# Omega on another issuing queue, the first loads in another order, and a planner that counts issue time: random-feature attention and two expert layers in fp32

## The chip, the cores and the metric

The kernel runs on one core of one Trainium2 chip. The metric is device time in microseconds of one execution. A core has TensorE (PE; matrix products and weight loads, PEld), VectorE (DVE), ScalarE (ACT), GpSimd (POOL) and SyncE (SP), and 16 DMA engines. Transfers are issued by an instruction on an engine's queue, here SyncE's and, for some, ScalarE's; in rows a queue is SPq or ACTq.

## The reference

```python
def _attn_ref(q, k, v, omega):            # q, k, v: (4, 8, 576, 64), omega: (128, 64)
    scale = 1.0 / np.sqrt(np.sqrt(D))
    def phi(x):                           # x = q * scale or k * scale
        proj = np.einsum('bhsd,md->bhsm', x, omega)
        h = proj - np.sum(x * x, axis=-1, keepdims=True) / 2.0
        return np.exp(h - np.max(h, axis=-1, keepdims=True)) / np.sqrt(m)
    kv = np.einsum('bhsm,bhsd->bhmd', phi(k * scale), v)
    z = np.sum(phi(k * scale), axis=2)
    num = np.einsum('bhsm,bhmd->bhsd', phi(q * scale), kv)
    den = np.einsum('bhsm,bhm->bhs', phi(q * scale), z)[..., None] + 1e-06
    return num / den
# x = attention output as (2304, 512)
gate = 1.0 / (1.0 + np.exp(-(x @ w_gate)))        # w_gate, w_val: (512, 1536)
x = (gate * (x @ w_val)) @ w_out                  # w_out: (1536, 512)
...
logits = x @ phi                                  # second layer: 8 experts of 4 slots
slot_input = softmax(logits, axis 0).T @ x
slot_out[e] = np.maximum(slot_input[e] @ w1[e], 0.0) @ w2[e]
return softmax(logits, axis 1) @ slot_out
```

## The kernel before, in words

Attention goes by 16 units of two heads. A unit has a transposed load of keys and queries (`QKTs`, two buffers; columns 0 to 511 keys, 512 to 639 the tails, the rest queries), a token-major load (`TOK`, one buffer, nine tiles: four of keys, one of tails, four of queries) and the values (`Vs`). `prep_first` and `prep_qk` square `TOK` and reduce the squares to one number for each row (`SQ`). `chunk_proj` multiplies 128 tokens at a time with Omega (`obf`, scaled once) into a PSUM bank, then VectorE subtracts the row's number and takes the minimum of the row (one instruction for a tile and head, which the rows of the trace call CUSTOM_DVE_ANT_0), and ScalarE takes the exponential. `chunk_kv`, `chunk_qT` and `chunk_num` make the attention output, which is stored in two float32r parts (`XT`).

The gated layer runs in 60 steps (`STEPS`: token block and 128 columns of the hidden layer), each three groups of twelve products: `ga`, `va` and the sum over the hidden layer in four banks `o0` to `o3`. Its weights come raw (`wall`, into four buffers `QS`), are converted by ScalarE, VectorE and GpSimd (`convert`), spilled to DRAM (`wscr`) and read again in later blocks (`load_w`, into `ws`); each is split into two float32r parts just before use (`split_w`). The second layer follows in chunks between the steps and at the end.

Nothing is issued in the order in which it is written. `Plan` records every instruction with its dependencies and a due time; `schedule` runs a list schedule over five engines, with the prices of `cost`, and this gives the order of each engine's queue. A recorded instruction may name two engines; the schedule picks one. SyncE's and ScalarE's queues run in order, so a transfer that waits for a buffer holds what stands behind it. All instructions are issued by one helper, so that all rows show its line, L403.

The lines that the change touches are the end of `cost` (before: an issue on SyncE costs 0.06, one on ScalarE what an elementwise instruction of that size costs), the table `PARTS` of `chunk_proj`, and the first lines that are recorded, L1109 to L1139. A call of `chunk_proj` takes one bank for a part of fewer than four tiles.

Of the kernel before, what the change touches and what calls it, by code (L numbers as in the profile page):

```python
# [101 lines left out]
class Plan:  # L102
# [95 lines left out]
    def cost(self, eng, method, kw, outs, ins):  # L198


        if method == "together":
            return TURN * (kw["parts"][0][2][0].ap[0][1] == 64) + sum(self.cost(eng, a[1], a[3], o, i)[0] for a, o, i in kw["parts"]), False
        o = outs[0] if outs else None
        n = self.free(o) if o is not None else 0
        if eng == "PE":
            if method == "transpose":
                return 0.109 * max(0.5, o.ap[0][1] / 128), False
            if ins[0].dtype == F32R:
                return (n + 32) / 2400.0, False
            if o.ap[0][1] == 32:  # L210
                return max(0.43 * n / 256, 0.055) / 4, False
            if o.ap[0][1] == 64:
                return max(n / 600.0, 0.21) / 2 + 0.12, False
            return (max(0.222, n / 600.0) / 2 if ins[0].ap[0][1] == 64 else max(0.222, n / 600.0)), False
        ni = max([n] + [self.free(a) for a in ins])
        psum = any(a.space == bass.MemoryType.PSUM for a in ins + outs)
        if eng == "ACT":
            return (0.07 if psum else 0.11) + 0.00083 * ni + 0.09 * sum(self.free(a) == 1 for a in ins), False
        if eng == "DVE":
            if method == "reciprocal":  # L220
                return 0.06 + 0.0054 * n, False
            if method == "tensor_tensor_reduce":
                return 0.075 + ni / 960.0, False
            if method == "tensor_reduce" or psum:
                return 0.067 + ni / 960.0, False
            if method in ("tensor_tensor", "scalar_tensor_tensor"):
                return 0.067 + ni / 960.0, True
            return 0.067 + ni / 1920.0, method != "memset"
        if eng == "POOL":
            return 0.1 + 0.00225 * ni, True  # L230
        return 0.06, False
# [174 lines left out]
def body(ctx, tc, nc, qkT, tok, von, omT, wall, phi, w1, w2, ident_d, srep_d, rrep_d, mask_d, out):  # L406
    plan = Plan(nc)
    PE, ACT, DVE, POOL, SP = (Eng(plan, e) for e in ("PE", "ACT", "DVE", "POOL", "SP"))
# [23 lines left out]
    def warm(x, n, tag):  # L432

        ps = bank(tag)[:, 0:x.shape[-1]]
        for _ in range(n):
            PE.matmul(ps, x[:, 0:128], x, start=True, stop=True)
# [7 lines left out]
    def stream(name, t):  # L444
        plan.t = t
        plan.lead = LEAD[name]
# [22 lines left out]
    def carve(reg, at, shape):  # L469
        n = int(np.prod(shape))  # L470
        names = "abcde"[:len(shape)]
        v = reg[:, at:at + n]
        if len(shape) == 1:
            return v
        return v.rearrange(f"p ({' '.join(names)}) -> p {' '.join(names)}",
                           **{c: d for c, d in zip(names, shape)})
# [14 lines left out]
    QKTs = [carve(g2, 1152 * k, [1152]) for k in range(2)]  # L491
    TOK = carve(g2, 2304, [9, 2, D])
    Vs = [carve(g3, 1280 * k, [NT, 2, 128]) for k in range(2)]
    QTF = carve(g3, 2560, [2, S])
    obf = carve(g3, 3712, [256])
    HKs = [carve(r, 0, [4, 2, M]) for r in (g4, q2)]
# [10 lines left out]
    def turn(lst, name):  # L507
        ring[name] = ring.get(name, -1) + 1
        return lst[ring[name] % len(lst)]
# [4 lines left out]
    def bank(tag=None):  # L514
        if tag is None:
            tag = turn(FLW, "fl") if wide[0] else "fl"
        tag = "fl" if tag in POOLED else tag
        return plan.tile(psp, [128, 512], F32, tag, NFL if tag == "fl" else 1, dyn=tag == "fl")
# [22 lines left out]
    def prep_first(a, e):  # L541

        w = SQW[:, 2 * a:2 * e, :]
        y = TOK[:, a:e].rearrange("p t h d -> p (t h) d")
        ACT.activation(out=w, in_=y, func=AF.Square)
        DVE.tensor_reduce(out=SQ[:, 2 * a:2 * e], in_=w, axis=AX.X, op=ALU.add)

    PARTS = {"K": (0, 4, HKs, 0, 0), "K0": (0, 2, HKs, 0, 0), "K1": (256, 2, HKs, 2, 4),
             "T": (512, 1, HTs, 0, 8), "Q": (640, 4, HQs, 0, 10), "Q0": (640, 2, HQs, 0, 10), "Q1": (896, 2, HQs, 2, 14)}

    def chunk_proj(u, i):

        if u >= NU:
            return
        c0, nt, hb, t0, g0 = PARTS[i]
        hb = hb[u % 2][:, t0:t0 + nt]
        x = QKTs[u % 2][:, c0:c0 + 128 * nt]
        if nt < 4:
            both = bank()[:, 0:256 * nt].rearrange("p (t h m) -> p t h m", h=2, m=M)
            ps = [both[:, :, h] for h in range(2)]  # L560
        else:
            ps = [bank()[:, 0:128 * nt].rearrange("p (t m) -> p t m", m=M) for _ in range(2)]

        def products():
            for t in range(nt):
                if nt < 4:
                    PE.matmul(both[:, t].rearrange("p h m -> p (h m)"), x[:, 128 * t:128 * t + 128], obf,
                              start=True, stop=True)
                    continue
                for h in range(2):  # L570
                    r = slice(64 * h, 64 * h + 64)
                    PE.matmul(ps[h][:, t], x[r, 128 * t:128 * t + 128], obf[r, 128 * h:128 * h + 128],
                              start=True, stop=True)

        plan.together(products, [SQ[:, g0:g0 + 2 * nt]], [hb])
        low = turn(MX, "mx")
        for h in range(2):
            for t in range(nt):
                g = 2 * t + h
                DVE.tensor_tensor_reduce(out=hb[:, t, h], in0=ps[h][:, t],  # L580
                                         in1=SQ[:, g0 + g:g0 + g + 1].to_broadcast([128, M]),
                                         scale=1.0 / 16.0, scalar=BIG, op0=ALU.add, op1=ALU.min,
                                         accum_out=low[:, g:g + 1])
        for h in range(2):
            for t in range(nt):
                g = 2 * t + h
                ACT.activation(out=hb[:, t, h], in_=hb[:, t, h], func=AF.Exp, scale=-1.0, bias=low[:, g:g + 1])
# [519 lines left out]


    stream("att", T0)  # L1109
    ACT.preload_act_table_set("natural_log_exp_and_others")  # L1110
    DVE.memset(g4[:, 0:256], 0.0)
    warm(g4[:, 0:256], W0N, "va")
    for h in range(2):
        r = slice(64 * h, 64 * h + 64)
        DVE.memset(obf[r, 128 * (1 - h):128 * (2 - h)], 0.0)
        SP.dma_start(out=obf[r, 128 * h:128 * h + 128], in_=omT[r])
    SP.dma_start(out=TOK[:, 0:2], in_=tok[0][:, 0:2])
    SP.dma_start(out=QKTs[0][:, 0:256], in_=qkT[0][:, 0:256])
    SP.dma_start(out=TOK[:, 2:5], in_=tok[0][:, 2:5])
    SP.dma_start(out=QKTs[0][:, 256:640], in_=qkT[0][:, 256:640])  # L1120
    SP.dma_start(out=QKTs[0][:, 640:1152], in_=qkT[0][:, 640:1152])
    SP.dma_start(out=TOK[:, 5:9], in_=tok[0][:, 5:9])
    SP.dma_start(out=QKTs[1], in_=qkT[1])
    SP.dma_start(out=Vs[0], in_=von[0])
    SP.dma_start(out=ident, in_=ident_d)
    DVE.memset(one_b, 1.0)
    DVE.memset(den_b, 1e-6)
    DVE.tensor_scalar(out=obf, in0=obf, scalar1=-16.0 * float(D ** -0.25), scalar2=None, op0=ALU.mult)
    prep_first(0, 2)
    chunk_proj(0, "K0")  # L1130
    prep_first(2, 5)
    prep_qk(0, 1)
    chunk_proj(0, "K1")
# [176 lines left out]
def build(nc, arrays):  # L1310
    args = [nc.dram_tensor(n, a.shape, mybir.dt.from_np(a.dtype), kind="ExternalInput").ap()
            for n, a in arrays.items()]
    args.append(nc.dram_tensor("out_0", (NTOK, DM), F32, kind="ExternalOutput").ap())
    with tile.TileContext(nc, schedule_with_timeline_sim=True) as tc:
        with ExitStack() as ctx:
            body(ctx, tc, nc, *args)
# [8 lines left out]
```

## Time and profile before

| | |
|---|---|
| median of 3 runs | 694.21 us (693.05 to 696.72) |
| the profiled execution, its own time | 696.61 us |
| its span, first to last instruction | 694.8 us |
| PE busy | 668.5 us, 96% of the span |
| DVE busy | 459.4 us, 66% |
| ACT busy | 433.1 us, 62% |
| POOL busy | 288.4 us, 42% |
| transfers | 139.49 MB, mean 201 GB/s |

The shares are means over the whole span. Stages differ: attention alone at first, then attention beside the first steps of the gated layer, then the gated layer alone with chunks of the second one, then the end of the second layer. A matmul counts as busy while it waits in the array's pipeline, so a busy PE is not PE at its peak.

### The profile page before, as it was taken

To read this page: it belongs to the slowest core of one execution; us is meant where nothing else is said; L and a number is where in the kernel's file an instruction comes from. 1 tells how busy PE (TensorE), PEld (TensorE's weight loads), DVE (VectorE), ACT (ScalarE), POOL (GpSimd) and SP (SyncE) were. 2 spreads that over 40 slices of the span, in tenths; PEclk is the share of its full clock that TensorE was granted. 3 is DMA by queue.
4 is the path that set the end of the run, shared out by engine and by line. 5 is a ranking of instruction groups with operands and counts; after the bars stand their busy time and mean duration, and the time that the engine had idled before them with its cause. 6 is when DMAs were issued, how large, how long until landed. Compare 5 with 4: busy or idle time off the path is not lost.

```text
span 694.8 us, 12218 instructions
## 1 busy us (share of the span) xinstructions
PE 668.5 (96%) x4217; PEld 535.4 (77%) x4217; DVE 459.4 (66%) x1304; ACT 433.1 (62%) x968; POOL 288.4 (42%) x244
## 2 busy tenths in 40 slices
PE   7899899999999999999999999999999999999993
PEld 5676577778787888888788888788888789998562
DVE  3899999899997476766566664566454335765221
ACT  5899788888787665765667675454444446764021
POOL 0565445575344334344444543444444444642000
PEclk9999999999999999999999999999999999999898
DMA  7989766777965345424353312689432338658996
GB/s 253 327 273 334 258 213 226 266 249 249 320 221 178 125 136 195 152 90 125 119 186 118 92 46 92 205 291 342 147 92 92 107 86 290 175 163 265 329 389 215
DMA packets 50125, 139.49 MB, mean 201 GB/s; under 512 B 5520, under 2 KB 11152, under 8 KB 50064
## 3 DMA queue, kind: packets, MB, share of 16 engines
q1 hardware_dynamic: 45456, 121.94, 52.9%
q10 hardware_dynamic: 4608, 16.78, 7.1%
q8 instruction: 33, 0.54, 0.3%
q14 instruction: 28, 0.23, 0.1%
HBM read 124.54 MB, written 14.16 MB: 200 GB/s over the span
## 4 chain that ended last, share of the span: by engine, by line
PE 79%; DVE 8%; DMA 5%; ACT 3%; issue 3%; SPq 1%; POOL 0%; POOLq 0%; ACTq 0%; DVEq 0%
PE o L403 25%; PE ga L403 20%; PE va L403 19%; PE fl L403 15%; DVE x2T L403 3%; DVE g L403 2%; DMA ws<-wscr 2%; DMA g<-in_wall 2%; DVE x L403 1%; ACT g L403 1%; DMA wscr<-x 1%; DMA g<-in_tok 1%; ACT ga_a L403 1%; SPq L403 1%; DVE gt L403 1%
## 5 line engine op out<-in xcount | busy, mean ns | idle before, releaser
L403 POOL TENSOR_TENSOR w<-ws,w 128x512 fp32r<-128x512 f32 x138 | 181.6, 1317 | 254.1 <-ACT w L403 156.4
L403 PE MATMUL ga<-XT,w 128*128 128x512 f32 (+1 forms) x720 | 168.5, 376 | 0.7 <-DVE ga_a L403 0.7
L403 PE MATMUL o<-gt,w 128*128 128x512 f32 (+1 forms) x720 | 167.8, 377 | 0.9 <-ACT w L403 0.8
L403 PE MATMUL va<-XT,w 128*128 128x512 f32 (+1 forms) x720 | 166.9, 375 | 0.0
L403 PEld LDWEIGHTS o<-gt,w 128*128 128x128 f32 x720 | 123.6, 189 | 26.5 <-issue 3.9
L403 PEld LDWEIGHTS va<-XT,w 128*128 128x128 f32 x720 | 123.8, 189 | 25.4 <-issue 4.1
L403 PEld LDWEIGHTS ga<-XT,w 128*128 128x128 f32 x720 | 123.6, 189 | 25.5 <-DVE ga_a L403 1.3
L403 ACT ACTIVATE w<-ws 128x512 fp32r<-128x512 f32 x108 | 67.8, 627 | 58.4 <-PE o L403 19.5
L403 PE MATMUL fl<-g,g 64*128 64x128 f32 (+4 forms) x686 | 84.1, 313 | 4.8 <-DVE g L403 4.2
L403 ACT ACTIVATE g<-g 128x128 f32<-128x128 f32 (+3 forms) x204 | 73.4, 410 | 15.3 <-DVE g L403 9.7
L403 ACT ACTIVATE ga_a<-ga_a 128x512 f32<-128x512 f32 (+1 forms) x120 | 69.9, 583 | 20.4 <-DVE ga_a L403 19.5
L403 PEld LDWEIGHTS fl<-g,g 64*128 64x128 f32 (+2 forms) x686 | 61.0, 183 | 26.7 <-DVE g L403 9.4
L403 ACT ACTIVATE ga_a<-ga 128x512 f32<-128x512 f32 (+1 forms) x60 | 33.2, 553 | 67.0 <-PE ga L403 66.8
L403 DVE SCALAR_TENSOR_TENSOR ga_a<-ga,ga_a 128x512 f32<-128x512 f32 (+1 forms) x60 | 38.1, 634 | 41.0 <-ACT ga_a L403 40.9
L403 DVE CAST w<-ws 128x512 fp32r<-128x512 f32 x54 | 23.1, 428 | 57.5 <-PE ga L403 37.5
L403 ACT ACTIVATE x2T<-g 128x512 f32<-128x512 f32 x72 | 45.5, 665 | 8.2 <-DVE x L403 7.8
L403 DVE TENSOR_TENSOR ga_a<-va,ga_a 128x512 f32<-128x512 f32 (+1 forms) x60 | 38.0, 634 | 15.5 <-ACT ga_a L403 9.9
L403 ACT ACTIVATE g1b<-g1b,g 128x128 f32<-128x128 f32 x128 | 40.5, 390 | 8.6 <-DVE g L403 8.6
L403 DVE TENSOR_SCALAR x2T<-x2T 128x512 f32<-128x512 f32 (+1 forms) x72 | 44.0, 627 | 1.0 <-ACT x2T L403 1.0
L403 DVE TENSOR_TENSOR gt<-ga_a,gt 128x512 fp32r<-128x512 f32 (+1 forms) x53 | 40.3, 760 | 2.3 <-ACT gt L403 1.3
L403 ACT ACTIVATE ga_a<-ga_a,one_b 128x512 f32<-128x512 f32 (+1 forms) x60 | 40.7, 678 | 1.4
L403 DVE TENSOR_TENSOR g<-fl,g 64x288 f32<-64x288 f32 (+3 forms) x61 | 29.3, 482 | 17.4 <-ACT g L403 16.5
(201 smaller groups left out, 787.7 us busy)
## 6 DMA issues: line engine op xcount, KB each, us to landing
ws<-wscr SPq DMA_DIRECT2D x42, 512.0 KB, 3.6
ws<-wscr SPq DMA_DIRECT2D x78, 256.0 KB, 2.8
g<-in_wall SPq DMA_DIRECT2D x36, 512.0 KB, 4.5
g<-in_von SPq DMA_DIRECT2D x16, 640.0 KB, 5.2
wscr<-x SPq DMA_DIRECT2D x36, 256.0 KB, 4.1
g<-in_qkT SPq DMA_DIRECT2D x15, 576.0 KB, 4.9
g<-in_tok SPq DMA_DIRECT2D x15, 576.0 KB, 5.0
g<-in_w ACTq DMA_DIRECT2D x16, 512.0 KB, 6.1
```

The costliest lines, as they stand in the source:

```text
L403: getattr(self.eng[e], method)(*a, **k)
```

## The change

Omega's two loads are issued on ScalarE's queue instead of SyncE's, ahead of the activation table load, which was ScalarE's first instruction. SyncE starts with the token-major load; the last four token tiles come one place earlier, before the last part of keys and queries; the second unit's key and query load comes after the values and the identity. The first part of the projection, two key tiles in one bank (`K0`), becomes two parts of one tile, with a bank each (`Ka`, `Kb`). In the planner a transfer's issue costs 0.5 on SyncE and 0.06 on any other engine.

```diff
@@ cost
+        if method == "dma_start":
+            return 0.5 if eng == "SP" else 0.06, False
         o = outs[0] if outs else None
@@ PARTS
+             "Ka": (0, 1, HKs, 0, 0), "Kb": (128, 1, HKs, 1, 2),
@@ body
     stream("att", T0)
-    ACT.preload_act_table_set("natural_log_exp_and_others")
     DVE.memset(g4[:, 0:256], 0.0)
     warm(g4[:, 0:256], W0N, "va")
+    SP.dma_start(out=TOK[:, 0:2], in_=tok[0][:, 0:2])
     for h in range(2):
         r = slice(64 * h, 64 * h + 64)
         DVE.memset(obf[r, 128 * (1 - h):128 * (2 - h)], 0.0)
-        SP.dma_start(out=obf[r, 128 * h:128 * h + 128], in_=omT[r])
-    SP.dma_start(out=TOK[:, 0:2], in_=tok[0][:, 0:2])
+        ACT.dma_start(out=obf[r, 128 * h:128 * h + 128], in_=omT[r])
     SP.dma_start(out=QKTs[0][:, 0:256], in_=qkT[0][:, 0:256])
     SP.dma_start(out=TOK[:, 2:5], in_=tok[0][:, 2:5])
     SP.dma_start(out=QKTs[0][:, 256:640], in_=qkT[0][:, 256:640])
+    SP.dma_start(out=TOK[:, 5:9], in_=tok[0][:, 5:9])
     SP.dma_start(out=QKTs[0][:, 640:1152], in_=qkT[0][:, 640:1152])
-    SP.dma_start(out=TOK[:, 5:9], in_=tok[0][:, 5:9])
-    SP.dma_start(out=QKTs[1], in_=qkT[1])
     SP.dma_start(out=Vs[0], in_=von[0])
     SP.dma_start(out=ident, in_=ident_d)
+    SP.dma_start(out=QKTs[1], in_=qkT[1])
+    ACT.preload_act_table_set("natural_log_exp_and_others")
...
-    chunk_proj(0, "K0")
+    chunk_proj(0, "Ka")
+    chunk_proj(0, "Kb")
```

The planner's new prices reach every queue. Three places follow. The first is the start of SyncE's queue. In these rows `g_78` holds `TOK` and `QKTs` (128x256, 128x384 and 128x512 are the parts of the first unit, 128x1152 a whole unit), `g_79` holds Omega and the values, `in_wall` are raw weights. Before:

```order
L403 DMA g_79<-in_omT 64x128 x2
L403 DMA g_78<-in_tok 128x256
L403 DMA g_78<-in_qkT 128x256
L403 DMA g_78<-in_tok 128x384
L403 DMA g_78<-in_qkT 128x384
L403 DMA g_78<-in_qkT 128x512
L403 DMA g_78<-in_tok 128x512
L403 DMA g_78<-in_qkT 128x1152
L403 DMA g_79<-in_von 128x1280
L403 DMA ident<-in_ident 128x128
L403 DMA g_79<-in_von 128x1280
L403 DMA g_78<-in_tok 128x1152
```

The same queue after the change:

```order
L405 DMA g_78<-in_tok 128x256
L405 DMA g_78<-in_qkT 128x256
L405 DMA g_78<-in_tok 128x384
L405 DMA g_78<-in_qkT 128x384
L405 DMA g_78<-in_tok 128x512
L405 DMA g_78<-in_qkT 128x512
L405 DMA g_79<-in_von 128x1280
L405 DMA ident<-in_ident 128x128
L405 DMA g_78<-in_qkT 128x1152
L405 DMA g_79<-in_von 128x1280
L405 DMA g_78<-in_tok 128x1152
L405 DMA g_75<-in_wall 128x1024 x2
```

Omega's two issues are gone, the 128x512 part of the tokens has moved from eighth to fifth, and the second unit's token load (128x1152) is now followed by two weight loads where four stood.

The second place is the start of ScalarE's queue. `g_78` 128x256, 128x384, 128x512 and 128x640 are squares of token tiles, `g_80` 128x128 exponentials of a tile and head, `fl` and `o` PSUM banks. Before:

```order
L403 ACT_TABLE_LOAD
L403 ACTIVATE g_78<-g_78 128x256
L403 ACTIVATE g_78<-g_78 128x384
L403 ACTIVATE g_80<-g_80 128x128 x18
L403 ACTIVATE g_80<-o_88 128x256
L403 ACTIVATE g_79<-o_90 128x2x256
L403 ACTIVATE g_79<-fl 128x2x256
L403 ACTIVATE g_79<-o_93 128x2x64
L403 ACTIVATE g_80<-fl,den_b 128x288
```

The same queue after the change:

```order
L405 DMA g_79<-in_omT 64x128 x2
L405 ACT_TABLE_LOAD
L405 ACTIVATE g_78<-g_78 128x256
L405 ACTIVATE g_78<-g_78 128x384
L405 ACTIVATE g_80<-g_80 128x128 x2
L405 ACTIVATE g_78<-g_78 128x512
L405 ACTIVATE g_80<-g_80 128x128 x16
L405 ACTIVATE g_80<-fl 128x256
L405 ACTIVATE g_79<-o_93 128x2x256
L405 ACTIVATE g_79<-o_94 128x2x64
L405 ACTIVATE g_78<-g_78 128x640
L405 ACTIVATE g_80<-o_100,den_b 128x288
```

The square of the last four token tiles (128x512) and that of the second unit's first five (128x640) have come from GpSimd to ScalarE, and one PSUM copy has gone to VectorE.

The third place is SyncE's queue late in the first blocks of the gated layer, where raw weights, spills (`wscr`) and reloads (`ws`, 128x1024 for the two input weights, 128x512 for the output weight) alternate. Before:

```order
L403 DMA wscr<-x_138 128x512
L403 DMA ws<-wscr 128x1024
L403 DMA g_75<-in_wall 128x1024
L403 DMA wscr<-x_138 128x512
L403 DMA ws<-wscr 128x512
L403 DMA g_75<-in_wall 128x1024
```

The same place after the change:

```order
L405 DMA ws<-wscr 128x1024
L405 DMA wscr<-x_139 128x512
L405 DMA g_75<-in_wall 128x1024 x2
L405 DMA wscr<-x_139 128x512
L405 DMA ws<-wscr 128x512
L405 DMA ws<-wscr 128x1024
```

Between the two reloads of one step stand two raw weight loads and two spills now, where one of each stood.

## Rows read from the trace of the kernel before

**Rows 1.** Busy time by stage: stretch, its length, then each engine's busy time.
```profile
0.00:20.00 20.00, 15.29 (x69) 11.62 (x70) 6.98 (x46) 10.46 (x27) 2.50 (x6) 1.00 0.79 269
20.00:150.00 130.00, 124.71 (x770) 90.28 (x769) 122.71 (x440) 114.44 (x297) 72.52 (x65) 1.00 0.77 265
150.00:210.00 60.00, 57.43 (x276) 46.71 (x274) 59.25 (x106) 49.05 (x98) 27.57 (x20) 1.00 0.77 258
210.00:625.00 415.00, 414.14 (x2415) 346.67 (x2416) 248.49 (x655) 244.07 (x514) 181.94 (x150) 1.00 0.48 152
```

**Rows 2.** The chain of waits at the start: start, duration, what.
```profile
4.54 6.02 DMA g<-in_tok
10.70 1.05 POOL g L403
...
13.09 7.00 DMA g<-in_wall
```

**Rows 3.** Timeline of SyncE's queue, first 12 us: start, duration, issue.
```profile
0.73 1.24 SPq L403 DMA_DIRECT2D g<-in_omT  x2
2.01 0.59 SPq L403 DMA_DIRECT2D g<-in_tok  x1
...
3.12 0.43 SPq L403 DMA_DIRECT2D g<-in_tok  x1
...
4.54 0.43 SPq L403 DMA_DIRECT2D g<-in_tok  x1
...
6.44 0.88 SPq L403 DMA_DIRECT2D g<-in_von  x1
11.76 0.33 SPq L403 DMA_DIRECT2D g<-in_tok  x1
```

**Rows 4.** Transfers of the first 40 us: GB/s by us; issue to landing in us.
```profile
GB/s 0 0 57 181 227 291 237 262 319 324 284 404 381 386 328 311 295 281 397 422 420 415 441 402 386 215 243 333 128 188 378 361 398 164 319 316 316 278 108 161
...
g<-in_qkT SPq DMA_DIRECT2D x1, 256.0 KB, 4.6
g<-in_tok SPq DMA_DIRECT2D x1, 256.0 KB, 6.0
...
g<-in_tok SPq DMA_DIRECT2D x1, 128.0 KB, 2.4
```

**Rows 5.** Timeline of the first 20 us, all engines; in brackets idle time and releaser.
```profile
0.73 1.28 ACT L403 ACT_TABLE_LOAD   x1 [0.73 <-PEq L1320]
...
5.38 2.05 PE L403 MATMUL fl<-g,g 128*128 128x256 f32 x4 [1.27 <-DVE g L403]
...
7.47 0.29 DVE L403 CUSTOM_DVE_ANT_0 g<-fl,g 128x128 f32<-128x128 f32 x1
...
18.39 1.25 POOL L403 TENSOR_TENSOR g<-g 128x640 f32<-128x640 f32 x1 [6.65 <-DMA g<-in_tok]
...
19.68 0.82 DVE L403 TENSOR_REDUCE g<-g 128x10 f32<-128x640 f32 x1 [5.31 <-POOL g L403]
```

**Rows 6.** Groups of instructions by shape, whole span: count, busy us, mean ns.
```profile
L403 DVE CUSTOM_DVE_ANT_0 x<-x2T 128x1024 uint16<-128x1024 uint16 x25 | 24.3, 971 | 0.1
L403 DVE CAST gt<-ga_a 128x512 fp32r<-128x512 f32 x37 | 23.9, 647 | 0.8
L403 DVE TENSOR_TENSOR w<-ws,w 128x512 fp32r<-128x512 f32 x24 | 18.0, 750 | 5.4 <-ACT w L403 4.5 <-issue 0.5
L403 DVE COPY g<-fl 128x512 f32<-128x512 f32 x13 | 8.9, 686 | 2.3 <-PE fl L403 2.2
L403 ACT ACTIVATE g<-g 128x512 f32<-128x512 f32 x8 | 5.0, 626 | 2.2 <-DVE g L403 1.3 <-issue 0.9
L403 ACT ACTIVATE g<-g 128x640 f32<-128x640 f32 x2 | 1.5, 732 | 0.7 <-DVE g L403 0.7
```

**Rows 7.** Waits of SyncE's queue: what it waited for: us, times, longest.
```profile
SPq L403 <- DVE x2T L403: 87.4, 39, 7.9
```

**Rows 8.** SyncE's loads of the tile ws: who waited for them (us, times).
```profile
  POOL w L403: 2.2, 1
  DVE w L403: 0.2, 1
```

## The prediction

> **What bounds the kernel now.** I read first the busy time by stage [rows 1]. From 210 to 625 us TensorE is busy 414.14 of 415 us: there the time is its own work, and nothing that arrives earlier shortens it; it can only start earlier. From 20 to 210 us VectorE is the fullest engine, 122.71 of 130 and 59.25 of 60 us, with TensorE at 124.71 and 57.43; both carry a backlog. In the first 20 us nobody is full: VectorE 6.98, ScalarE 10.46, TensorE 15.29 us. So idle time in the first 20 us is paid in full at the end, unless a later stage has a bound of its own.
>
> Then the chain of waits [rows 2]. It starts on SyncE's queue, runs through one transfer of 6.02 us (the last four tiles of the token-major load, `TOK[:, 5:9]`), GpSimd's square of it, and from there into a 7.00 us weight load. The queue itself [rows 3] shows why: SyncE issues its first load at 0.73 us, needs about 0.6 us for each of the first and 0.43 to 0.47 us from start to start later, and issues nothing between 7.3 and 11.76 us, because the next unit's token load overwrites `TOK` and waits for that square. The timeline [rows 5] shows what it costs: the square ends at 11.75 us and VectorE reduces it next; the next unit's square starts at 18.39 us, when its load has landed, 6.63 us after its issue, and VectorE, idle 5.31 us, gets its reduction at 19.68 us. The first product waits until 5.38 us.
>
> **The change, part by part.**
> Omega to ScalarE's queue. Two issues leave SyncE: its first token load moves from 2.01 to 0.73 us, 1.28 us [rows 3]. Omega keeps its issue times, now on an idle engine. The activation table load goes behind it, so by the same issue times it begins at about 2.0 instead of 0.73 us and, at its 1.28 us [rows 5], ends at 3.3; the first square needs a token load issued at 0.73 us, and that load lands 2.4 us after issue [rows 4], at 3.1 us, where it lands at 4.4 now. Cost 0.2 us on a square that still starts 1.1 us sooner: nothing on the path. Without that cover it would be 1.3 us.
>
> Order of the first loads. `TOK[:, 5:9]` was the eighth issue of the queue (4.54 us) and is now the fifth, which is issued at 3.12 us today [rows 3]. The 256 KB load that stands where it will stand among the large loads (the last part of the key and query load) landed 4.6 us after issue, `TOK[:, 5:9]` itself 6.0 us [rows 4]. So it lands at 3.1 + 4.6 = 7.7 us, at worst 9.1, instead of 10.56. Its square is on ScalarE in the new order: 0.63 us [rows 6] in place of 1.05 [rows 2]. ScalarE's two exponentials ahead of it are of tile 0, long done. The square ends at 8.4 us (worst 9.8) instead of 11.75, and the next token load is issued then: 3.4 us sooner (worst 1.9).
>
> That gain doesn't arrive whole, because the transfers are then bound by traffic. All that is issued up to and with that load is, by the shapes in the code, 3712 KB or 3.8 MB. The figures of [rows 4], one per us, add to 4.7 MB when it lands today at about 18.3 us: 0.9 MB of the four weight loads issued behind it went first. In the new order two weight loads stand behind it, then a load that waits for TensorE, so I take between 0.45 and 0.9 MB. The same sums, 4.25 to 4.7 MB, are reached at 16.9 to 18.3 us today and 1.28 us sooner after the change: 15.6 to 17.0, a gain of 1.3 to 2.7. I take 2.0. The square behind it moves from GpSimd (1.25 us [rows 5]) to ScalarE (0.73 us [rows 6]): 0.5 more. So the second unit's reduction comes at about 17.2 us instead of 19.68: 2.5 us, bounds 1.8 and 3.2. What lies ahead has room: the first unit's last reduction on VectorE moves from 11.8 to about 8.5 us, and what queues behind it moves too.
>
> The Trainium skill, DMA: Bandwidth & Descriptors, section "Issuing engines are not separate DMA queues", says that transfers issued from different engines run on the same 16 DMA engines and interleave, so that several issuers save only issue time. It speaks against the move of Omega as a gain in bandwidth. The trace agrees as far as it goes: from 11 us on the figures of [rows 4] stay between 281 and 422 GB/s with one queue issuing. By that rule alone the change would give its 1.28 us of issue time and no more.
>
> The last part of the key and query load stands one place later now; it may land at 3.6 + 6.0 = 9.6 us instead of 8.6. VectorE then still has the reductions of earlier tiles queued ahead of its own, at 0.29 us for one half tile [rows 5]: 0, at most the 1 us if that queue were empty.
>
> A bank for each of the first two key tiles. VectorE's first row reduction at 7.47 us waits for both tiles of one bank, 2.05 us of product [rows 5]; with a bank each it needs one tile, half of that. Its key load, the fourth issue today, is the second now, so the first product can start about 1.3 us sooner, near 4.1 us, and VectorE near 5.2. That work sits in front of the wait for the second unit's load, so it is hidden by it: 0. If that load came at once, it would be worth up to 2 us.
>
> The counted issue. SyncE's issue costs 0.5 us in the plan instead of 0.06, ScalarE's 0.06 instead of the price of an elementwise operation. This reorders every engine. TensorE's matmuls are the same 3376. Counted in the orders up to the nineteenth gate step, about where VectorE stops being the bound, VectorE loses five PSUM copies (0.69 us each) and three conversion adds (0.97), 6.3 us, and gains four subtractions (0.75), two casts of the gated value and two of weights (0.65 at most each), 5.6 us [rows 6]. Net 0.7 us less; 0 if what waits there is TensorE, up to 2 with the small copies, which I leave out. I take 0.7 us. ScalarE gains four squares of 128x640 (0.73 each) and some of the copies.
>
> Sum: 2.5 + 0.7 = 3.2 us. Span 694.8 - 3.2 = 691.6 us; the profiled execution's own time 696.61 becomes 693.4. It lies 2.4 us above the median of the runs, 694.21, which becomes 691.0 us. About 0.5% (3.5 us) is what a measurement of this kernel tells from no change, so this lies just inside it.
>
> **Rivals.**
> *Carried, and the new order closes more.* VectorE idles 7.3 us and TensorE 5.3 us between 20 and 150 us [rows 1]. An order planned with true issue times may place loads sooner and close half of VectorE's part, 3.6 us: 687.4. For it: the chain is made of loads that come late. Against: after 20 us SyncE mostly waits for buffers, not for its issue.
>
> *Not carried.* The start gains only the issue time, 1.28 us, or the stage up to 150 us hides the rest, since ScalarE is busy 114.44 of its 130 us and now gets more: 692.9 to 694.2. The first of these is also what the Trainium skill's rule on issuing engines, above, gives.
>
> *Slower: a reload queued behind weight loads.* SyncE's queue is in order. In the new one, a reload of the output weights (`ws`, 128x512) stands behind two raw weight loads, where one stood before. Each of these waits for a buffer that VectorE's conversion must free; such waits reached 7.9 us [rows 7]. If the reload comes that late and the step waits, the time is 691.0 + 7.9 = 698.9. It decides once the reload is later than its slack. Against it: of 120 reloads two were waited for, 2.4 us in all [rows 8].
>
> **How the numbers follow.** Forecast case 0.50, with its own range 689.0 to 692.9 (3.2 + 2.0, and 1.3 with nothing from the order); a little over half of it lies past the 0.5% bound at 690.7. Closing more 0.18, not carried 0.15, slower 0.17. Faster by over 0.5%: 0.26 + 0.18 = 0.44. Within: 0.24 + 0.15 = 0.39. Slower: 0.17. The range 686.5 to 696.5 leaves out the dear half of the slower case and the tail of the gain.
>
> **What would show it.** The first token load issued near 0.7 us and the first product near 4.1; `TOK[:, 5:9]` landed by 7.7 to 9.1; the next token load issued near 8.4; the second unit's reduction on VectorE near 17.2; TensorE's full stretch beginning about 3 us sooner, with the same length of 415 us. I am wrong if the start is 2.5 us ahead and TensorE's idle time between 20 and 250 us has grown by as much, if ScalarE is what VectorE waits for between 20 and 100 us, or if waits for `ws` appear before the weight splits.

## The result, and the profile after

The change made the kernel slower. The median is 703.02 us (698.60 to 705.04, 9 runs) against 694.35 us (693.05 to 697.96, 9 runs); the ratio, taken over all runs and not of the two medians (which lie 8.7 us apart), is 1.0095, with a 95% interval of 1.0071 to 1.0118: 6.6 us slower, at least 4.9, where 3.2 us faster was forecast, and outside the forecast's range.

The profiled execution of the changed kernel is its fastest (698.60 us, span 696.7), so its span lies only 1.9 us above before's 694.8. Part of the rest is the clock at the end: between 640 and 661 us the granted clock was 0.84 before and 1.00 after. The steps in the middle compare better. TensorE's seventeenth gate step begins at 247.70 us before and at 252.83 after.

First the start. SyncE's queue after (start, duration, issue), which answers to [rows 3]:

```profile
0.74 0.41 SPq L405 DMA_DIRECT2D g<-in_tok  x1
...
2.71 0.43 SPq L405 DMA_DIRECT2D g<-in_tok  x1
...
5.10 0.56 SPq L405 DMA_DIRECT2D g<-in_von  x1
7.93 0.33 SPq L405 DMA_DIRECT2D g<-in_tok  x1
```

The timeline of the other engines, for [rows 5]:

```profile
1.96 1.28 ACT L405 ACT_TABLE_LOAD   x1 [1.96 <-issue]
...
5.00 1.22 PE L405 MATMUL fl<-g,g 128*128 128x256 f32 x2 [0.89 <-DVE g L405]
...
14.85 0.74 ACT L405 ACTIVATE g<-g 128x640 f32<-128x640 f32 x1
...
15.62 0.82 DVE L405 TENSOR_REDUCE g<-g 128x10 f32<-128x640 f32 x1 [1.43 <-ACT g L405]
```

The first token load goes out at 0.74 us, `TOK[:, 5:9]` at 2.71, the next unit's token load at 7.93 instead of 11.76, and the second unit's reduction comes at 15.62 instead of 19.68 us. All of this is as soon as forecast or sooner, except the first product: 5.00, not 4.1. The chain of waits says why (start, duration, what):

```profile
0.74 0.55 ACTq L405
...
1.32 3.20 DMA g<-in_omT
```

Omega's second half landed 3.20 us after its issue at 1.32, and the scaling on VectorE had to wait for it.

So the start is 4 us ahead. Now the busy time by stage, for [rows 1] (stretch, length, then PE, PEld, DVE, ACT, POOL, granted clock, DMA share, GB/s):

```profile
0.00:20.00 20.00, 16.90 (x81) 12.79 (x82) 11.04 (x68) 14.23 (x37) 2.23 (x7) 1.00 0.87 323
20.00:150.00 130.00, 123.30 (x753) 88.69 (x754) 114.43 (x409) 114.94 (x296) 66.81 (x60) 1.00 0.75 256
150.00:210.00 60.00, 57.16 (x272) 45.78 (x271) 57.37 (x112) 47.13 (x94) 26.36 (x20) 1.00 0.79 262
210.00:625.00 415.00, 412.87 (x2383) 344.46 (x2382) 239.49 (x637) 246.02 (x519) 182.85 (x152) 1.00 0.46 150
```

VectorE, nearly full before, is now idle 15.57 of 130 us between 20 and 150, where it was idle 7.29. It has less to do, and TensorE still does 1.41 us less than before in that stretch, 0.27 less in the next and 1.27 less in the last. TensorE's timeline after shows some of the places; in brackets the idle time and who ended it:

```profile
53.53 0.47 PE L405 MATMUL ga<-XT,w 128*128 128x512 f32 x1 [1.28 <-DVE XT L405]
63.25 2.47 PE L405 MATMUL fl<-g,g 128*128 128x128 f32 x20 [1.70 <-ACT ga_a L405]
...
215.82 0.39 PE L405 MATMUL ga<-XT,w 128*128 128x512 f32 x1
217.87 1.71 PE L405 MATMUL fl<-g,g 64*128 64x128 f32 x16 [1.66 <-DVE g L405]
219.51 2.97 PE L405 MATMUL ga<-XT,w 128*128 128x512 f32 x7
222.28 1.59 PE L405 MATMUL fl<-g,g1b 128*128 128x128 f32 x8
```

The wait at 217.87 stands in the fourteenth step (`ga` at 215.82 is its first gate product). Behind that product stands a projection of attention work (`fl`, 16 products), which waits 1.66 us for VectorE, and the step's other eleven gate products, which `after_ga13` below draws with no wait, stand behind it. VectorE's own timeline there:

```profile
214.27 0.68 DVE L405 SCALAR_TENSOR_TENSOR x2T<-g,x2T 128x512 int32<-128x512 int32 x1
...
215.66 1.78 DVE L405 CUSTOM_DVE_ANT_0 x<-x2T 128x1024 uint16<-128x1024 uint16 x1
217.37 0.93 DVE L405 TENSOR_TENSOR g<-fl,g 64x288 f32<-64x288 f32 x2
```

Two instructions of weight conversion, the second an add of 1.78 us, stand ahead of the attention instruction at 217.37 that frees the bank `fl`. Before, that add stands behind the attention instruction, and the 16 products have no wait:

```profile
215.90 0.93 DVE L403 TENSOR_TENSOR g<-fl,g 64x288 f32<-64x288 f32 x2
216.87 0.81 DVE L403 CUSTOM_DVE_ANT_0 x<-x2T 128x1024 uint16<-128x1024 uint16 x1
```

What follows the wait is read from the granted clock (the third number from the end of a row):

```profile
210.00:220.00 10.00, 8.24 (x45) 6.33 (x44) 9.77 (x13) 5.38 (x12) 4.89 (x5) 1.00 0.36 110
220.00:230.00 10.00, 10.00 (x59) 8.36 (x58) 5.36 (x36) 6.60 (x18) 2.82 (x3) 0.83 0.53 192
```

A mean of 0.83 over 10 us is 3.4 us at half the full clock, the lower of its two levels, a loss of 1.7 us. Before, the same two stretches show 1.00 and 1.00, with TensorE busy 9.73 and 10.00.

The remaining signs that the prediction named: loads of `ws` were waited for 5.2 us in five waits instead of 2.4 in two [rows 8], and SyncE waited less for conversions:

```profile
SPq L405 <- DVE x2T L405: 66.3, 33, 4.7
```

### The profile page after: what moved, and what is told of

Same layout as the page of the kernel before. It is cut to its first block, busy times and chain, and to the rows that moved or that the text cites. A ratio compares the mean times of both kernels' runs of the same rounds, so it can differ in the third digit from the quotient of the medians.

```text
span 696.7 us, 12215 instructions
## 1 busy us (share of the span) xinstructions
PE 668.9 (96%) x4217; PEld 535.8 (77%) x4217; DVE 447.9 (64%) x1290; ACT 440.2 (63%) x984; POOL 284.1 (41%) x242
## 4 chain that ended last, share of the span: by engine, by line
PE 78%; DVE 9%; ACT 5%; issue 3%; DMA 2%; POOL 1%; POOLq 0%; ACTq 0%; SPq 0%; DVEq 0%
PE o L405 24%; PE ga L405 20%; PE va L405 19%; PE fl L405 16%; DVE x2T L405 3%; ACT g L405 2%; DVE g L405 1%; DVE x L405 1%; ACT ga_a L405 1%; DVE gt L405 1%; DMA wscr<-x 1%; ACT XT L405 1%; DVE ga_a L405 1%; DVE g1b L405 1%; DMA g<-in_tok 1%
## 5 line engine op out<-in xcount | busy, mean ns | idle before, releaser
L405 POOL TENSOR_TENSOR w<-ws,w 128x512 fp32r<-128x512 f32 x136 | 178.1, 1310 | 257.2 <-ACT w L405 155.4
L405 PE MATMUL ga<-XT,w 128*128 128x512 f32 (+1 forms) x720 | 170.5, 379 | 2.3 <-DVE XT L405 1.3
L405 PE MATMUL fl<-g,g 64*128 64x128 f32 (+3 forms) x698 | 86.6, 311 | 6.2 <-DVE g L405 4.2
L405 ACT ACTIVATE g<-g 128x128 f32<-128x128 f32 (+4 forms) x207 | 75.1, 417 | 9.8 <-DVE g L405 6.6
L405 POOL TENSOR_TENSOR XT<-g,XT 128x64 fp32r<-128x64 f32 (+2 forms) x45 | 31.4, 709 | 23.3 <-ACT XT L405 23.0
```

What stands on the lines that cost most here:

```text
L405: getattr(self.eng[e], method)(*a, **k)
```

## The experiments

The rival theories at the start. A: the gain of the start is real, and the order that the counted issue makes loses it again. B: the new front itself costs. C: any fresh order of this planner costs, whatever the reason for drawing it; the issue prices have no guilt of their own. C stands so only from `redraw` on, put up after the first four runs were known: in the expectation of `hold_order` C is that a lead is absorbed, in those of `front_only`, `cost_only` and `price45` that an order lands by chance to either side. The table holds all runs: the ratio to the kernel before with its interval, the start of TensorE's seventeenth gate step in the timeline, and TensorE's busy time in the first 20 us and from 20 to 250 us. "Held" is the order of before.

| run | order | ratio (95%) | step 17 | PE 0 to 20 | PE 20 to 250 |
|---|---|---|---|---|---|
| before | | 1 | 247.70 | 15.29 | 221.86 |
| after | fresh | 1.0095 (1.0071, 1.0118) | 252.83 | 16.90 | 218.71 |
| `hold_order` | held | 0.9956 (0.9939, 0.9974) | 244.00 | 17.49 | 222.62 |
| `hold_omega` | held | 0.9986 (0.9966, 1.0006) | 245.22 | 16.48 | 222.61 |
| `hold_tok` | held | 0.9993 (0.9973, 1.0012) | 246.99 | 14.84 | 222.53 |
| `hold_squares` | held | 0.9962 (0.9942, 0.9982) | 244.37 | 17.23 | 222.61 |
| `front_only` | fresh | 1.0104 (1.0071, 1.0138) | 253.72 | 15.40 | 220.01 |
| `cost_only` | fresh | 1.0077 (1.0052, 1.0103) | 253.52 | 15.26 | 220.30 |
| `price45` | as after | 1.0094 (1.0066, 1.0123) | 255.25 | 17.19 | 218.49 |
| `redraw` | fresh | 1.0092 (1.0069, 1.0115) | 250.67 | 15.87 | 220.84 |
| `redraw_pool` | fresh | 1.0096 (1.0061, 1.0130) | | | |
| `redraw_late` | fresh from about 95 us | 1.0126 (1.0098, 1.0154) | 251.72 | 15.29 | 219.24 |
| `redraw_front` | as `redraw` | 1.0074 (1.0044, 1.0103) | 249.05 | 17.38 | 220.52 |
| `after_ga13` | after, one piece moved | 1.0065 (1.0042, 1.0087) | 251.66 | 15.41 | 219.03 |

**The front in the held order (`hold_order`).** The kernel before, with the first loads of the change but without its `Ka` and `Kb`; the finished order is edited just before it is issued:

```diff
+        steps = [x[2] for x in self.schedule()]
+        om0, om1, t0, q0, t2, q2, q6, t5, u1, v0, idn = [x for x in steps if x[0] == "SP"][:11]
+        table = next(x for x in steps if x[1] == "preload_act_table_set")
...
+        steps[k + 1:k + 1] = [q0, t2, q2, t5, q6, v0, idn, u1, table]
+        steps = [t0] + [("ACT",) + x[1:] if x is om0 or x is om1 else x for x in steps]
```

> The kernel before, planned as before, with only the first loads changed when the plan is issued: Omega's two loads on ScalarE's queue, the activation table load behind them, and SyncE's nine first loads in the order of the change. All else keeps its engine and place; the square of `TOK[:, 5:9]` stays on GpSimd. Theory A (the gain of the start is real, and it is the planner's other order behind it that loses it again): the second unit's reduction on VectorE about 3 us sooner than 19.68, and the time 0.996, between 0.993 and 0.998 (some 691.5 us against 694.35). Theory B (it is the new front itself that costs: loads that come together sooner, Omega late on its new queue): at or over 1.000, up to 1.009. Theory C (a lead at the start is absorbed before 250 us, whatever the order): the start sooner and the time within 0.999 to 1.001.

Measured: 692.20 us against 694.69, 0.9956, as A had it; B falls, and so does the C of this expectation, that a lead is absorbed. The next unit's token load goes out at 7.75 us, and every step of TensorE from the second to the last is 3.7 us ahead of before's profile. This is the clean test of the prediction's main step: idle time saved in the first 20 us arrives at the end in full when nothing else moves. The busy times (first 20 us, then 20 to 250 us) show it:

```profile
0.00:20.00 20.00, 17.49 (x84) 13.30 (x84) 10.49 (x65) 13.59 (x37) 3.30 (x7) 1.00 0.89 323
20.00:250.00 230.00, 222.62 (x1263) 170.29 (x1263) 207.72 (x611) 190.78 (x451) 118.08 (x101) 1.00 0.72 240
```

The changed kernel, with nearly the same start, in the second stretch:

```profile
20.00:250.00 230.00, 218.71 (x1216) 165.48 (x1217) 196.19 (x586) 185.97 (x441) 108.66 (x92) 0.99 0.70 236
```

**Half a change each (`front_only`, `cost_only`), and a nearby price (`price45`).** `front_only` is the changed kernel without the two lines in `cost`; `cost_only` is the kernel before with them; `price45` has 0.45 for SyncE's issue.

> The changed kernel without the two lines that price an issue; the planner then orders all instructions anew by the old prices, with the new front. Theory A (the counted issue makes the order that loses): 0.994 to 0.998. Theory B (the front costs): about 1.009. Theory C (any new order by this planner can land some us to either side): no sure sign, anything from 0.990 to 1.010, and TensorE's step times differ from before's all over the first 230 us.

> The kernel before with nothing but the two lines that price an issue; the front is as before. Theory A (the counted issue makes the order that loses 7 us or more between 25 and 230 us): 1.010 to 1.015, since the start's lead of 4 us is gone too. Theory B (the front costs): 0.998 to 1.000. Theory C (any new order lands by chance): 0.990 to 1.010.

> The changed kernel with SyncE's issue at 0.45 us in the plan instead of 0.5: the trace shows starts 0.43 to 0.47 us apart, so this price is no less true. Theory A and B: within 0.003 of the changed kernel, 1.006 to 1.013. Theory C (the order is a draw, and the loss belongs to this one draw): over 0.004 away from the changed kernel to either side, with the stall of TensorE at 210 to 223 us gone or elsewhere.

Measured: 1.0104, 1.0077 and 1.0094; A's ranges for the first two are missed. `front_only` has no counted issue and loses as much: A's culprit falls. It shares with `cost_only` only that the planner ordered everything anew. `price45` turned out to be no new draw: its order is that of the changed kernel but for one instruction each on TensorE, ScalarE and SyncE, so it says nothing on C. It is a second look at the changed kernel's order, and its seventeenth step came 2.4 us later in its profile than in after's: so much can one profiled execution differ. Some 1.7 of this is the clock, at 0.83 between 60 and 70 us, where after has 1.00.

**Fresh orders for no reason (`redraw`, `redraw_pool`, `redraw_late`).** The kernel before with one number of the plan touched:

```diff
-HOP = 0.16
+HOP = 0.17
```

`redraw_late` has 0.15; `redraw_pool` keeps 0.16 and has `0.1 + 0.0023 * ni` for GpSimd in place of `0.00225`.

> The kernel before with the planner's latency between engines (`HOP`) at 0.17 us instead of 0.16; the front and all prices of issues are as before. The order is drawn anew from the second unit on, about as far from before's as with the counted issue alone; no row of the trace makes one of the two values the better one. Theory A (what the counted issue or the new front tells the planner is what spoils the order): 0.998 to 1.002. Theory C (a fresh order by itself costs, because the order of before leaves TensorE and VectorE fewer gaps than this planner's draws usually do): 1.004 to 1.012, with TensorE's busy time up to 250 us about 1.5 us below before's 237.2.

> The kernel before with the plan's price for GpSimd's work per element at 0.0023 instead of 0.00225, 2% up; front and issue prices as before. A second fresh order, from the second unit on. Theory C (a fresh order by itself costs): 1.004 to 1.012, TensorE's busy time up to 250 us 0.5 to 2 us under before's 237.2. If the first redraw was a bad one by chance: 0.997 to 1.003.

> The kernel before with the planner's latency between engines at 0.15 us instead of 0.16. The engines' orders agree with before's up to some 95 us and part from there. Theory C: a loss again, a smaller one, since less of the stage is drawn anew: 1.002 to 1.008, with TensorE's steps as before up to 95 us and behind from there. If chance goes both ways: 0.996 to 1.002.

Measured: 1.0092, 1.0096 and 1.0126. The sign is C's in all three, though `redraw_late` lost more than its 1.002 to 1.008: a change that means nothing costs as much as the change under study, with before's front and before's prices of issues. (`redraw_pool`'s profile isn't used: in that one execution the large products took 1.6 us each, and the ratio is that of the other six.)

The loss isn't all in one place. From the start of the 56th gate step to that of the 60th, with the same products, `redraw` takes 22.3 us (609.75 to 632.08), `redraw_late` 22.1 and `redraw_front`, below, 22.9, against 19.3 in before (607.58 to 626.92), in the changed kernel and, within 0.1, in each other profile. So these draws lose some 3 us there that the changed kernel doesn't; at the seventeenth step `redraw` and `redraw_late` are 3.0 and 4.0 us behind before's profile, the changed kernel 5.1. Why the last steps take longer is open.

`redraw_late` is the clearest for the middle, for up to about 95 us its queues are those of before but for a swap of a few transposes on TensorE. Its TensorE timeline behind that:

```profile
201.22 0.72 PE L403 MATMUL fl<-g,g 128*128 128x288 f32 x2 [2.69 <-DVE g L403]
...
214.97 1.71 PE L403 MATMUL fl<-g,g 64*128 64x128 f32 x16 [1.92 <-DVE g L403]
```

The second of these is the wait that the changed kernel has at 217.87. The same 16 products wait for VectorE in each profile of a fresh order but `after_ga13`'s, where they were moved: 0.82 us in `front_only`, 0.16 in `cost_only`, 1.68 in `price45`, 0.94 in `redraw`, 0.93 in `redraw_front`. Before and the held orders have no such wait. In `cost_only` it is small and the loss is as large, so this one wait isn't the whole cause.

`redraw_late` shows one thing more. With before's own order at the start, its second gate step came 1.37 us sooner than in before's profile, and its next token load was issued sooner:

```profile
10.26 0.33 SPq L403 DMA_DIRECT2D g<-in_tok  x1
```

Before's profile has 11.76 there [rows 3]. Nothing in the program differs up to that point: `TOK[:, 5:9]` landed 4.5 us after issue instead of 6.0 [rows 4]. With the same first loads it took 4.6 us in `redraw` and 5.5 in `cost_only`. The profile on which the prediction rests had a late start, by up to 1.5 us.

**One piece of the order put back (`after_ga13`).** In the changed kernel's finished order, the fourteenth step's gate products are drawn together ahead of the attention work:

```diff
+        part = steps[1820:1873]
+        ga = [x for x in part if x[0] == "PE" and x[1] == "matmul" and x[2][0].tensor.name.startswith("ga_3")]
+        steps[1820:1873] = ga + [x for x in part if not any(x is y for y in ga)]
```

> The changed kernel with one piece of TensorE's order changed: at the fourteenth step the eleven gate products that stood behind three chunks of attention work stand ahead of them; nothing else moves. If the wait of 1.66 us at 217.87 and the stretch of half clock at 220.0 are one cause of the loss: no such wait, the clock at 1.00 between 210 and 230 us, and 1.7 to 3.4 us less than the changed kernel: 1.0045 to 1.007 against before. If the work only waits elsewhere, for VectorE is behind: 1.0095, as the changed kernel.

Measured: 1.0065 against 1.0095, within what was expected; the intervals overlap, and the profile carries the verdict. The granted clock of the runs agrees: its median is 0.990 in the changed kernel and 0.994 here. TensorE's timeline:

```profile
216.63 2.88 PE L409 MATMUL ga<-XT,w 128*128 128x512 f32 x12
219.44 1.16 PE L409 MATMUL fl<-g,g 64*128 64x128 f32 x16
221.95 1.16 PE L409 MATMUL fl<-g,g1b 128*128 128x128 f32 x8 [1.35 <-DVE g L409]
```

and the same two stretches of 10 us:

```profile
210.00:220.00 10.00, 9.53 (x48) 7.54 (x50) 9.74 (x15) 6.19 (x14) 4.15 (x4) 1.00 0.34 116
220.00:230.00 10.00, 8.59 (x65) 7.27 (x62) 6.96 (x38) 7.60 (x21) 4.00 (x5) 1.00 0.66 205
```

The projection no longer waits, a later chunk waits 1.35 us instead, since VectorE is behind in any case, and the clock stays at 1.00. The steps, 0.8 us behind those of after up to here, are 1.2 ahead from here on: 2.0 us, of which the half clock is 1.7.

**The two halves of the front (`hold_omega`, `hold_tok`).** The held order, with only Omega's loads and the table load moved, or only `TOK[:, 5:9]`, the values and the identity moved ahead.

> The kernel before in its own order; only Omega's two loads go to ScalarE's queue, with the activation table load behind them. By the terms of the prediction: the first token load at 0.73 us, 1.28 sooner, all that follows on SyncE's queue 1.28 sooner, and the second unit's reduction and the end by as much: 693.1 us, 0.998. If the lead of 3.7 us in the held order comes from this part: 0.995. If it comes from the order of the token and key loads alone: 0.999 to 1.001.

> The kernel before in its own order, Omega on SyncE as before; only `TOK[:, 5:9]` is loaded ahead of the last key and query part, and the first unit's values and the identity ahead of the second unit's keys. By the terms of the prediction (2.5 less 1.28): 1.2 us sooner, 0.998. If the square of this tile is all that holds the second unit's load: 2 to 2.5 us sooner, 0.9965. If the traffic holds it: 0.999 to 1.001.

Measured: 0.9986 and 0.9993, both intervals with 1 inside, while both halves together give 0.9956. Omega's move is worth about 1.0 us (0 lies within its interval), near the 1.28 of issue time that the prediction gave it. The Trainium skill, DMA: Bandwidth & Descriptors, section "Issuing engines are not separate DMA queues", says that several issuing engines save only the time of issuing. `hold_omega` agrees, with 1.0 us of 1.28. For `TOK[:, 5:9]` the prediction's terms leave 1.2 us, and alone it gives 0.9993, which the expectation has for "if the traffic holds it". Its profile fits that: the next token load goes out at 9.32 us, 0.94 sooner than in `redraw_late`, but lands 7.1 us after issue instead of 5.9, and the second unit's reduction comes at 17.89 instead of 17.56. It isn't clean, since the granted clock was 0.91 over its first 20 us, which alone is 1.8 us lost. Beside Omega's move the same piece shows its 1.2 us: `hold_order` differs from `hold_omega` in nothing else, and its seventeenth step is 1.22 us sooner (244.00 against 245.22), in one profile of each.

**The lead in a bad order (`redraw_front`), and the squares (`hold_squares`).** `redraw_front` joins `redraw` and the edit of `hold_order`. `hold_squares` is `hold_order` with two squares on ScalarE instead of GpSimd.

> The first redraw (latency 0.17) with the first loads changed when the plan is issued, as in the held order; the rest of the redrawn order stays. If the lead of the start and the loss of the order are two terms that add: 1.0092 less 0.0044, that is 1.004 to 1.006, with TensorE's steps some 3.7 us ahead of the redraw's. If an order that leaves gaps swallows the lead: 1.008 to 1.010.

> The held order with the new first loads, and two squares moved from GpSimd to ScalarE: that of `TOK[:, 5:9]` (1.04 us on GpSimd) ahead of the first exponential, where ScalarE is idle for 2.04 us, and that of the second unit's first half (1.25 us) behind three copies. If these squares are on the path to the second unit's reduction: 15.99 becomes 15.2 to 15.6 us and TensorE's steps gain 0.3 to 0.8 us: 0.9945 to 0.9955. If TensorE is what that part waits for: steps as in the held order, 0.9956.

Measured: 1.0074, between the two cases. The steps tell more: from the second step to the 56th `redraw_front` is 1.6 to 1.8 us ahead of `redraw` (at the seventeenth 249.05 against 250.67), and 1.2 at the last. So a bad order doesn't swallow a lead that has come as far as the second step, as the case of two terms that add has it. That the lead is 1.6 and not 3.7 is in part because `redraw`'s own start was as early as that of `redraw_late` (its next token load went out at 10.34 us); 0.7 us of it stay open. `hold_squares`: 0.9962, no gain over `hold_order` that can be measured.

The best version, with `hold_squares` no different, is therefore `hold_order`: 0.9956 against before, where the changed kernel has 1.0095.

## Why the prediction was wrong

**The step that failed** is "The counted issue": "Net 0.7 us less; 0 if what waits there is TensorE, up to 2 with the small copies". It priced a new order by the busy time that it takes from VectorE, gave that a lower bound of no loss, and put at nothing what a new order itself may cost. It also laid the reordering to the prices alone; the new front draws a new order by itself (`front_only`). The busy time did fall: over the whole span the adds of the conversions are 22 instead of 25, as counted, and the copies 10 instead of 13, where five fewer had been counted [rows 6]:

```profile
L405 DVE CUSTOM_DVE_ANT_0 x<-x2T 128x1024 uint16<-128x1024 uint16 x22 | 20.4, 930 | 0.1
...
L405 DVE COPY g<-fl 128x512 f32<-128x512 f32 x10 | 6.9, 687 | 2.1 <-PE fl L405 1.8
```

Over the whole span VectorE is busy 447.9 us instead of 459.4, and the kernel is slower. In one place it is shown that what counts is who stands ahead of whom: with VectorE's order untouched, `after_ga13` took back 2.0 us, 1.7 of them half clock. That the rest of the loss is of this kind is a reading. Between 20 and 250 us TensorE did 3.15 us less work than before, and 3.91 less than in the held order. That is the condition that the prediction set itself: "TensorE's idle time between 20 and 250 us has grown by as much". By the ratios the new order costs 1.0095 less 0.9956, 0.0139 or 9.7 us. By the steps it is 8.8 us (252.83 less 244.00). Of these, rows show 3.9 us of TensorE's idle time from 20 to 250 us, 0.6 in the first 20, and 1.7 of half clock; 2.6 us don't show as idle time. They lie in TensorE's busy time: the same number of products of each shape stands ahead of that step in both kernels, busy for 238.4 us in the changed kernel and 234.1 in the held order, 1.7 of the difference being the half clock. What held them is open.

**The start was right.** Term by term: the first token load at 0.73 (0.74), the next one near 8.4 (7.93), `TOK[:, 5:9]` landing by 7.7 to 9.1 (4.0 us after 2.71, so 6.7), the table load hidden (it ended at 3.24). The sum of 2.5 us compares with 3.1 us by the held order's ratio (0.0044 of 694.7; 1.8 to 4.2 by its interval). In the profiles it looks larger, 4.06 at the reduction, since the one profile of before was 1.5 us late. The first product's 4.1 was wrong by 0.9: Omega, not the key load, came last. Two details of the prediction don't hold, without weight in the sum: the figures of [rows 4] stay between 281 and 422 GB/s from 11 to 20 us only, and no profile shows 3376 matmuls. Each counts 4217, the same for both kernels, which is what the argument needed.

**"Paid in full at the end"** was right too, and the clause "unless a later stage has a bound of its own" wasn't what undid it: in `hold_order` the lead stays whole to the last step, in `redraw_front` all but 0.4 us of it.

**The rivals.** "Closing more" expected true issue times to close gaps; VectorE's gaps doubled. "Slower" had the right sign at 698.9, with another mechanism: waits for `ws` rose by 2.8 us only, and the largest single one was 2.8 us, on GpSimd, not 7.9. "Not carried" supposed that a later stage hides the start; it does not. What was missing is a rival that is not about this change at all: an order drawn anew by this planner is 0.8 to 1.3% slower than the one at hand. That is shown by five fresh draws besides the changed kernel's own, three of which changed nothing of meaning. They don't all lose in the same places, as the last steps of the redraws show. Why before's order is the better one is not shown. The likeliest reading is that it was kept as the best of many draws, and no run here tells that from a planner that happens to fit these numbers.

## What to carry to other kernels

Where a planner sets the order, an edit to a load or a price is two changes: the edit, and a fresh order of everything behind it. Cost them apart: hold the finished order and edit it for the first, and draw an order with a meaningless change for the second; here these were 3.1 us gained and some 6 to 9 us lost. Here a sum of busy times bounded neither; look for in-order heads that wait while ready work stands behind them. And a start that is read from one profile can be off by more than the term at stake: here 1.5 us, in a transfer's landing.

## What the runs showed of the hardware

A wait of 1.66 us on TensorE at 216 us was followed by 3.4 us at half clock from 220 us on; with the wait moved and cut to 1.35 us the clock stayed at 1.00 (`after_ga13`), and before had one of 1.71 us at 85.93 us with the clock at 1.00 over the 30 us around it. So a short wait may cost as much again, and doesn't always. Where `redraw_late` waited 2.69 and 1.92 us within 14 us, the clock fell as well (210 to 220 us):

```profile
210.00:220.00 10.00, 7.99 (x41) 6.24 (x40) 9.37 (x27) 5.76 (x15) 5.32 (x6) 0.86 0.54 174
```

The same 256 KB load, issued at the same time in the same queue, landed after 6.0 us in one execution and after 4.5 us in another. And Omega's 32 KB halves, 2.0 us from issue to landing on SyncE's queue in `redraw_late` (at most 2.2 in the other profiles that have them there), took 2.8 us (median of two) on ScalarE's beside SyncE's loads.
